# Three token tiles instead of two in the first rows of a feed-forward, and x of the third on another queue

## The chip, the cores and the metric

The kernel runs on one core of one Trainium2 chip. The metric is the device time of one execution in microseconds (us), the median over runs. A time shown with a profile is that of one profiled execution.

The engines are named as the profile names them: PE is TensorE's matmul stream and PEld its weight loads, DVE is VectorE, ACT is ScalarE, POOL is GpSimd, SP is SyncE, which here issues most DMAs. ACTq, POOLq and SPq are the queues on which those engines issue DMAs. Each engine runs its instructions in program order and waits at an instruction until its operands are ready, so what stands behind a waiting instruction waits too.

## The reference

Layer norm without weights over x (2048 tokens of 512 features), then the sum of three things: x, a diagonal complex state-space layer (S5) over the normalised tokens, and a SwiGLU feed-forward of them with 1376 hidden units. Inputs and output are bf16.

```python
x = A_x
xn = _layernorm(x, axis=-1)
return x + _A_ref(xn, ...) + _B_ref(xn, B_w_gate, B_w_up, B_w_down)

def _layernorm(x, axis=-1, eps=1e-5):
    m = jnp.mean(x, axis=axis, keepdims=True)
    v = jnp.var(x, axis=axis, keepdims=True)
    return (x - m) / jnp.sqrt(v + eps)

# _A_ref: Lam_bar = exp(dt * Lam);  B_bar = ((Lam_bar - 1) / Lam)[:, None] * Bmat
#         h_t = Lam_bar * h_(t-1) + B_bar @ xn_t
#         y_t = 2 Re(Cmat @ h_t) + xn_t * Dskip
# _B_ref: (silu(xn @ w_gate) * (xn @ w_up)) @ w_down
```

## The kernel before

**Tiles and chunks.** The 2048 tokens are 16 tiles of 128, four to a chunk, so four chunks of 512. Each chunk goes through the same stages on PE: `bproj` (L387, the projection of the normalised tokens by B, real and imaginary), the gate and up products of the feed-forward (L462 with hidden units on the partitions), `gateup_last` (L555, the 96 hidden units that don't fill a tile of 128), `out_ffn` (L630, the down product), `out_rest` (L620, its part for the last hidden units) and `out_ssm` (L643, the C product, added into the same PSUM bank). DVE does a rotation, a scan over time and a rotation back for each chunk (L397 to L411, L429), and the elementwise products of gate and up (L493, L541).

PE needs the tokens with features on the partitions. For chunks 1 to 3 they are normalised on DVE (chunk 1, L207) or ACT (chunks 2 and 3, L212) into `xn`, and one transposing DMA on SP (`xT_dma`, L262) turns all four tiles of a chunk into `xnT`. `bproj` of the chunk is the first to need it.

**The head.** Chunk 0 can't wait for that. Its first tiles are put through gate and up before the mean and deviation are known, with tokens as the stationary operand (`sw_mm`, L506): PE transposes raw x against an identity matrix (L237), adds minus the mean to the same PSUM bank by a matmul of the tokens' sums (`cT_mean`, L245), and ACT and DVE copy the result to `xcT` in bf16 (L252). The deviation comes in later, as the scale of the copies out of PSUM. Tiles 0 and 1 do this together, row by row of the weights as their DMAs land: `row_mm(0, k)` are the four matmuls of up for the rows k of the weights, `row_mm(1, k)` the gate's. Each weight row is a DMA of 256 KB on SP. Tile 2 comes later: it is centred on DVE (L226) once its statistics are there, and transposed into a bank `t2`. Tile 3 waits for a transposing DMA of its normalised tokens. What is left of the gate and up products of tiles 0 to 3 (hidden groups 0, 1 and 2 of 512, 512 and 352 units) is done in a loop over (group, tile), near L815, with L805 for the last group, whose gate and up share a bank.

**The parameters.** Lambda and log_dt come in as rows and are transposed on PE in one matmul (`prm_transpose`, L278), copied by DVE (`prm_copy`, L282), and lead to the tables of the rotation.

**The order of the work.** The program's order is written out by hand. Matmuls and what empties their banks are emitted in place. Statistics, normalisations, rotations, scans and table work go into a list, the backlog, with a cost in us for each, and `pump(us)` emits from the front of it as much as the credit `owed` allows. It is called beside each group of matmuls with about the time that PE needs for them. `need(tag)` emits all up to the last entry of a tag. Products are not in the backlog: they are emitted by `multiply(keep)`, which lowers the credit by 0.65 each. So the credit decides how the backlog's work stands between the products on DVE, between the copies out of PSUM on ACT, and so when each normalisation is done.

```python
def pump(us):
    owed[0] += us
    while backlog and owed[0] >= backlog[0][0] * 0.5:
        step()
```

The same mechanism holds the skip path at the end: `skip_op` makes `xr` on ACT (L592) and multiplies it on DVE (L600), for tiles 0 to 11, ahead of the back rotation of chunk 3. `out_ssm` copies a tile of chunks 0 to 2 out of PSUM on ACT into `res` (L652), which a DMA adds to the output in DRAM; for chunk 3 DVE adds it to x and the skip path (L646) and it is stored.

Of the kernel before, what the change touches and what calls it, by code (L numbers as in the profile page):

```python
# [11 lines left out]
BF16 = mybir.dt.bfloat16  # L12
ALU = mybir.AluOpType
# [10 lines left out]
def kernel(  # L24
# [17 lines left out]
    nc = tc.nc  # L42
    _, L, D = A_x.shape
# [6 lines left out]
    NCH = L // CW  # L50
    TPC = CW // 128
    KD = D // 128
# [15 lines left out]
    const = ctx.enter_context(tc.tile_pool(name="const", bufs=1))  # L68
# [9 lines left out]
    def bank(shape=(128, CW), dtype=F32):  # L78
        return psum.tile(list(shape), dtype, name="ps")
# [4 lines left out]
    x_v = A_x[0].rearrange("(n p) d -> p n d", p=128)  # L84
# [5 lines left out]
    xall = const.tile([128, NT, D], BF16, name="xall")  # L90
    xnT = const.tile([128, NCH, KD, CW], BF16, name="xnT")
# [38 lines left out]
    nc.scalar.dma_start(out=xall[:, 1, :], in_=x_v[:, 1, :])  # L130
# [43 lines left out]
    mv = const.tile([128, NT, 2], F32, name="mv")  # L174
# [30 lines left out]
    def norm_dve(n):  # L205
        c, i = divmod(n, TPC)
        nc.vector.tensor_scalar(out=xn_tile(c)[:, :, i, :], in0=by_k(xall[:, n, :]), scalar1=mv[:, n, 0:1],  # L207
                                scalar2=rstd[:, n:n + 1], op0=ALU.subtract, op1=ALU.mult)
# [8 lines left out]
    xcT, xc = CF[:, 0], CF[:, 1]  # L217
# [5 lines left out]
    sums = const.tile([128, 2], BF16, name="sums")  # L223

    def center(i):
        nc.vector.tensor_scalar(out=xc[:, i, :], in0=xall[:, i, :], scalar1=mv[:, i, 0:1], scalar2=None, op0=ALU.subtract)  # L226
# [5 lines left out]
    pair = [[[bank() for _ in range(2)] for _ in range(2)] for _ in range(2)]  # L232
    warm = pair[0][0][1]
    raw = [pair[0][1] + pair[1][0], pair[1][1] * 2]

    def cT_mm(ps, src, k, first, stop):
        nc.tensor.matmul(ps[:, k * 128:(k + 1) * 128], lhsT=src[:, k * 128:(k + 1) * 128], rhs=ident[:], start=first,  # L237
                         stop=stop)
# [5 lines left out]
    def cT_mean(i, *ks):  # L244
        nc.tensor.matmul(by_k(raw[i][ks[0]][:])[:, ks[0]:ks[-1] + 1:HK], lhsT=sums[:, i:i + 1].to_broadcast([128, 128]),  # L245
                         rhs=minus_mean[:, None, :].to_broadcast([128, len(ks), 128]), start=False, stop=True)

    def raw_copy(i, k):
        cT_copy(V.tensor_copy if k % 2 else nc.scalar.copy, raw[i][k], i, k, k + 1)

    def cT_copy(copy, ps, i, k0=0, k1=KD):
        copy(out=xcT[:, k0:k1, i * 128:(i + 1) * 128], in_=by_k(ps[:, k0 * 128:k1 * 128]))  # L252

    def runs(ap):
        return ap.rearrange("p k (i t) -> p (k i) t", t=128)
# [18 lines left out]
    V = nc.vector  # L274

    def prm_transpose():
        pp = bank()[:, 0:128]
        nc.tensor.matmul(pp, lhsT=prm_rows[:], rhs=ident[:], start=True, stop=True)  # L278
        return pp

    def prm_copy(pp):
        V.tensor_copy(out=prm[:].rearrange("p t q -> p (t q)"), in_=pp[:, 0:3 * NQ])  # L282

    def exp_pool(out, in_):
        nc.gpsimd.tensor_tensor(out=out, in0=e_t[:], in1=in_, op=ALU.pow)

    def params_a():
        V.tensor_tensor(out=dre[:], in0=dt_t[:], in1=lre, op=ALU.mult)
        exp_pool(r_t[:], dre[:])
        V.scalar_tensor_tensor(out=ws2[:, 0, :], in0=dt_t[:], scalar=INV_2PI, in1=lim, op0=ALU.mult, op1=ALU.mult)  # L290
# [212 lines left out]
    def sw_mm(ps, groups, gi, i, k0=0, k1=KD):  # L503
        a, b = fgroups[gi]
        for k in range(k0, k1):
            nc.tensor.matmul(ps[:, 0:(b - a) * 128], lhsT=tokens(i, k), rhs=groups[gi][:, k, 0:(b - a) * 128],  # L506
                             start=(k == 0), stop=(k == KD - 1))
# [14 lines left out]
    def sw_up(gi, i, psu):  # L522
        key, h, w = u_home(gi, i)
        if key not in u_pair:
            u_pair[key] = up_p.tile([128, 2, CW], BF16, name="u2")
        nc.scalar.activation(out=u_pair[key][:, h, 0:w], in_=psu[:, 0:w], func=ACT.Copy, scale=sw_scale(i))

    def sw_out(gi, i, psg, psu):
        a, b = fgroups[gi]
        key, h, w = u_home(gi, i)  # L530
        sw_gate(gi, i, psg)
        if psu is not None:
            sw_up(gi, i, psu)
        if h == 1:
            if key[-3:] == "g01":
                g = g0[:, 0:b, i, :].rearrange("p (h f) d -> p h f d", h=2)
                u = u_pair[key][:].rearrange("p h (f d) -> p h f d", d=128)
            else:
                g = g0[:, a:b, i - 1:i + 1, :]
                u = u_pair[key][:, :, 0:w].rearrange("p i (f d) -> p f i d", d=128)  # L540
            products.append(lambda: V.tensor_tensor(out=g, in0=g, in1=u, op=ALU.mult))  # L541
# [185 lines left out]
    dummy(warm, 4, CW)  # L727
    dummy(warm, 5, 128)
    nc.vector.tensor_scalar(out=minus_mean[:], in0=ident[:], scalar1=-1.0 / D, scalar2=None, op0=ALU.mult)
    for i in range(2):  # L730
        sum_dve(i, sums[:, i:i + 1])
    raw_mm(0)
    for k in range(HK):
        cT_mean(0, k)
        raw_copy(0, k)
    raw_mm(1)
    for k in range(HK, KD):
        cT_mean(0, k)
    for k in range(HK):
        cT_mean(1, k, k + HK)  # L740
        raw_copy(1, k)
    for k in range(HK, KD):
        raw_copy(0, k)
    for k in range(HK, KD):
        raw_copy(1, k)

    def row_mm(which, k):
        for i in range(2):
            for gi in range(2):
                sw_mm(pair[which][i][gi], (U, G)[which], gi, i, k, k + 1)  # L750

    for k in range(KD):
        row_mm(0, k)
    for i in range(2):
        ln_stats(i)
        ln_rstd(i, i + 1)
    for gi in range(2):
        for i in range(2):
            sw_up(gi, i, pair[0][i][gi])
    for n in range(2):  # L760
        norm_dve(n)
    row_mm(1, 0)
    pp = prm_transpose()
    ln_stats(2)
    center(2)
    ln_rstd(2, 3)
    ln_stats(3)
    ln_rstd(3, 4)
    prm_copy(pp)
    exp_pool(dt_t[:], ldt)  # L770
    for k in range(1, SW):
        row_mm(1, k)
    t2 = bank()
    for k in range(KD):
        cT_mm(t2, xc[:, 2, :], k, k == 0, k == KD - 1)
    cT_copy(nc.scalar.copy, t2, 2)
    row_mm(1, SW)
    for i in range(2):
        sw_out(0, i, pair[1][i][0], None)
    norm_dve(SW)  # L780
    xT0_dma(SW, TPC)
    norm_dve(2)
# [6 lines left out]
    for i in range(2):  # L789
        sw_out(1, i, pair[1][i][1], None)  # L790
    tables = table_ops()
    stats1, norm1 = ln_rest(1, False)
    queue("tables", tables[:1])
# [151 lines left out]
```

## Time and profile before

| What | us |
|---|---|
| median of 3 runs (lowest, highest) | 177.92 (177.83, 178.49) |
| the profiled execution's own time | 178.12 |
| its span in the profile | 176.0 |
| PE busy | 171.0 |
| DVE busy | 157.4 |
| ACT busy | 102.3 |
| POOL busy | 27.1 |

The span is the time from the first to the last record of the profile; the execution's own time has the start and end around it. The page gives shares of the span per engine, the busy tenths in 40 slices of 4.4 us each, the chain that ended last, followed backwards, and the costliest groups of instructions by line. The timeline lists the instructions of a stretch, one line for several of a kind: start, time from the first start to the last end, engine, line of the kernel, operation, output from input, count, and in brackets how long the engine stood idle before and what released it. In the list of DMA issues the last number is the time from issue to landing.

### The profile page before, as it was taken

What the parts mean: (1) busy time and instruction counts of PE and PEld (TensorE: products, weight loads), DVE (VectorE), ACT (ScalarE), POOL (GpSimd) and SP (SyncE); (2) the same over time, 40 slices, a digit from 0 to 9 for tenths busy, and PEclk for the clock granted to TensorE, in tenths of its full rate; (3) what the DMA queues carried; (4) which work ended last, traced back from release to release, by engine and by line L of the source; (5) the groups of instructions that cost most, each with busy time, mean ns of one, the idle gap of its engine ahead of it and who ended that gap; (6) DMA issues with size and microseconds to landing.
All of it is one profiled execution on the core that took longest, in us unless ns stands there. A gap on an engine that the chain in (4) does not pass through costs nothing.

```text
span 176.0 us, 2435 instructions
## 1 busy us (share of the span) xinstructions
PE 171.0 (97%) x878; PEld 82.0 (47%) x894; DVE 157.4 (89%) x260; ACT 102.3 (58%) x188; POOL 27.1 (15%) x36
## 2 busy tenths in 40 slices
PE   8899999999999999999999999999999999999993
PEld 5444445564444464444444444446444444444542
DVE  3767999999999999999999999999999999589642
ACT  3179589794996689976044362014666652983100
POOL 5234110022000000000302500014100000530700
PEclk9999999999999999999999999999999999999999
DMA  5998969999999300220005830006310000597741
GB/s 152 370 342 80 194 110 181 303 202 293 169 207 274 115 4 0 50 61 0 2 4 111 94 34 0 0 4 68 53 22 0 0 4 0 70 164 124 93 89 60
DMA packets 34027, 18.05 MB, mean 103 GB/s; under 512 B 24512, under 2 KB 32832, under 8 KB 33888
## 3 DMA queue, kind: packets, MB, share of 16 engines
q1 hardware_dynamic: 30272, 14.39, 35.0%
q0 software_dynamic: 3456, 3.28, 14.6%
q10 hardware_dynamic: 288, 0.23, 0.4%
q8 instruction: 7, 0.11, 0.3%
q14 instruction: 4, 0.03, 0.1%
HBM read 8.33 MB, written 5.24 MB: 77 GB/s over the span
## 4 chain that ended last, share of the span: by engine, by line
PE 94%; DMA 3%; issue 1%; SPq 0%; ACT 0%; DVE 0%; ACTq 0%
PE ps L462 29%; PE ps L630 20%; PE ps L643 16%; PE ps L387 16%; PE ps L506 7%; PE ps L555 3%; DMA wu<-in_B_w_up_dram 3%; PE ps L805 2%; PE ps L620 2%; ACT u L489 0%; SPq L122 0%; SPq L128 0%; DVE xall L646 0%; PE ps L237 0%; PE ps L278 0%
## 5 line engine op out<-in xcount | busy, mean ns | idle before, releaser
L429 DVE TENSOR_TENSOR_SCAN g<-r_t,car,u 128x512 bf16<-128x512 f32 x24 | 28.8, 1263 | 0.0
L643 PE MATMUL ps<-CF,wt 128*128 128x512 bf16 (+2 forms) x133 | 28.2, 366 | 0.2
L387 PE MATMUL ps<-xnT,BT 128*128 128x512 bf16 x125 | 28.1, 379 | 0.2
L630 PE MATMUL ps<-wd_sb,guT 128*128 128x512 bf16 (+2 forms) x129 | 26.5, 362 | 0.1
L462 PE MATMUL ps<-xnT,wu 128*128 128x512 bf16 x94 | 24.5, 379 | 0.2
L462 PE MATMUL ps<-xnT,wg 128*128 128x512 bf16 x93 | 24.3, 379 | 0.1
L389 ACT CAST u<-ps 128x512 bf16<-128x512 f32 x32 | 17.8, 591 | 5.0 <-PE ps L387 4.1
L489 ACT CAST u<-ps 128x512 bf16<-128x512 f32 x30 | 17.8, 592 | 4.8 <-PE ps L462 4.8
L643 PEld LDWEIGHTS <-wt 128*128 128x128 bf16 x136 | 12.9, 98 | 15.0 <-DVE xall L600 0.4
L387 PEld LDWEIGHTS <-BT 128*128 128x128 bf16 x128 | 12.5, 98 | 14.9 <-DMA BT<-in_A_B_re_dram 0.3
L630 PEld LDWEIGHTS <-guT 128*128 128x128 bf16 x130 | 12.4, 98 | 13.8
L199 POOL TENSOR_TENSOR rstd<-ve,neg_half 128x1 f32<-128x1 f32 (+1 forms) x7 | 7.0, 1001 | 73.0 <-DVE ve L198 72.6
L652 ACT CAST res<-ps 128x512 bf16<-128x512 f32 x12 | 6.9, 582 | 18.5 <-PE ps L643 18.5
L592 ACT ACTIVATE xr<-xall,nb,rstd 128x512 bf16<-128x512 bf16 x16 | 11.8, 804 | 8.7 <-DVE xall L600 5.0
L653 POOL DMA_DIRECT2D out_dram<-res x12 | 10.5, 1043 | 35.6 <-ACT res L652 30.0
L462 PEld LDWEIGHTS <-wu 128*128 128x128 bf16 x96 | 9.4, 98 | 11.3
L488 ACT ACTIVATE guT<-ps 128x512 bf16<-128x512 f32 x20 | 12.1, 604 | 4.0 <-PE ps L462 3.6
L462 PEld LDWEIGHTS <-wg 128*128 128x128 bf16 x96 | 9.3, 98 | 10.6
L212 ACT ACTIVATE xn<-xall,nb,rstd 128x512 bf16<-128x512 bf16 x8 | 6.3, 816 | 8.8 <-DVE nb L202 8.8
L189 DVE BATCH_NORM_STATS2 stats<-xall 128x6 f32<-128x512 bf16 x16 | 10.8, 675 | 0.6 <-DMA xall<-in_A_x_dram 0.6
L462 PE MATMUL ps<-xnT,w_end 128*128 128x512 bf16 x47 | 10.8, 379 | 0.1
L397 DVE TENSOR_TENSOR pm<-g,c 128x2048 bf16<-128x2048 bf16 x8 | 9.8, 1222 | 0.1
(132 smaller groups left out, 235.3 us busy)
## 6 DMA issues: line engine op xcount, KB each, us to landing
out_dram<-in_A_x_dram SPq DMA_DIRECT2D x8, 192.0 KB, 3.2
out_dram<-res POOLq DMA_DIRECT2D x12, 128.0 KB, 3.1
out_dram<-xall POOLq DMA_DIRECT2D x3, 512.0 KB, 6.4
wd_sb<-in_B_w_down_dram SPq DMA_DIRECT2D x1, 1280.0 KB, 7.8
wu<-in_B_w_up_dram SPq DMA_DIRECT2D x4, 256.0 KB, 4.9
wg<-in_B_w_gate_dram SPq DMA_DIRECT2D x4, 256.0 KB, 5.5
xall<-in_A_x_dram SPq DMA_DIRECT2D x1, 1024.0 KB, 7.0
xall<-in_A_x_dram SPq DMA_DIRECT2D x1, 512.0 KB, 6.1
```

What stands on the lines that cost most here:

```text
L189: nc.vector.bn_stats(out=stats[:, n, 0, :], in_=xall[:, n, :])
L387: nc.tensor.matmul(ps[:] if c else by_k(ps[:]), lhsT=BT[:, part, k, q * 128:(q + 1) * 128], rhs=xnT[:, c, k, :] if c else xnT0[:, k], star ...
L389: nc.scalar.copy(out=u_tiles[c][:, part, q, :], in_=ps[:])
L429: V.tensor_tensor_scan(out=g()[:, part, q, :], data0=r_t[:, q:q + 1].to_broadcast([128, CW]), data1=u_tiles[c][:, part, q, :], initial=ini ...
L462: nc.tensor.matmul(ps[:fs, lo:hi], lhsT=wslice(groups, fi, k), rhs=xnT[:, c, k, lo:hi], start=(k == 0), stop=(k == KD - 1))
L488: nc.scalar.activation(out=gu(c, fi, fi + 1)[:fs, 0, :], in_=psg[:fs], func=ACT.Silu)
L489: nc.scalar.copy(out=u_pair[c][:fs, fi % 2, :], in_=psu[:fs])
L506: nc.tensor.matmul(ps[:, 0:(b - a) * 128], lhsT=tokens(i, k), rhs=groups[gi][:, k, 0:(b - a) * 128], start=(k == 0), stop=(k == KD - 1))
L592: nc.scalar.activation(out=box["xr"][:], in_=xall[:, n, :], func=ACT.Identity, scale=rstd[:, n:n + 1], bias=nb[:, n:n + 1])
L630: nc.tensor.matmul(o_tiles[n, b][:, 0:hi - lo], lhsT=gu(c, fi, fi + 1)[:, 0, i * 128:(i + 1) * 128], rhs=wd_sb[:, fi, lo:hi], start=(fi == ...
L643: nc.tensor.matmul(o[:, 0:hi - lo], lhsT=w_tiles[c][:, part, q, i * 128:(i + 1) * 128], rhs=CF[:, part, q, lo:hi], start=False, stop=(part ...
L653: nc.gpsimd.dma_start(out=out_v[:, n, lo:hi], in_=res[:, lo:hi], accum_op=ALU.add)
```

## The change

The first three tiles go through the first rows together, where before it was two.

- **x of tile 2** is issued second on ACT's queue, right after x of tile 1. Before, it was issued on SP between the second and third gate rows.
- **Raw transposes.** Tiles 0 to 2 are all transposed raw, four matmuls each into one bank, and ACT copies them to `xrT` in SBUF in halves (six copies). The sums' matmul is one per tile (`mean_mm`) and writes minus the mean to a bank of its own. DVE adds the two into `xcT` (`centered`, nine instructions), so the subtraction that stood in PSUM is now in SBUF. The centring of tile 2, its bank `t2` and its four transposes are gone.
- **Up rows.** Row 0 of up is emitted in pieces between the centred columns, rows 1 to 3 for three tiles each, six matmuls. The gates follow tile by tile, all rows of a tile together.
- **Parameters.** The transpose of the parameters stands behind row 2 of up (`k == HK`), and `prm_copy` between the statistics of tile 0 and those of tiles 1 to 3.
- **The loop** over (group, tile) loses (0, 2) and (1, 2), with the `pump` beside each.

```diff
@@
-    nc.scalar.dma_start(out=xall[:, 1, :], in_=x_v[:, 1, :])
+    for i in (1, 2):
+        nc.scalar.dma_start(out=xall[:, i, :], in_=x_v[:, i, :])
     nc.scalar.preload_act_table_set("silu_and_others")
...
     for k in range(HK):
         load_row(nc.sync, wg01, wg_v, k)
-    nc.sync.dma_start(out=xall[:, 2, :], in_=x_v[:, 2, :])
     load_row(nc.sync, wg01, wg_v, HK)
@@
+    upb0 = [bank() for _ in range(2)]
+    raw = [bank() for _ in range(SW)]
+    low01, low2 = bank(), bank()
+    upb = [upb0, raw[0:2], [raw[2], bank()]]
+    gateb = [[low01, low2], upb[0], upb[1]]
+    warm = upb0[0]
+    xrT = xnT[:, NCH - 2]
...
     def raw_mm(i):
         for k in range(KD):
-            cT_mm(raw[i][k], xall[:, i, :], k, all(p is not raw[i][k] for p in raw[i][:k]), False)
+            cT_mm(raw[i], xall[:, i, :], k, k == 0, k == KD - 1)
...
+    def raw_copy(i, h):
+        k0, k1 = h * HK, (h + 1) * HK
+        nc.scalar.copy(out=xrT[:, k0:k1, i * 128:(i + 1) * 128], in_=by_k(raw[i][:, k0 * 128:k1 * 128]))
+
+    def mean_of(i):
+        return low2[:, 0:128] if i == SW - 1 else low01[:, i * 128:(i + 1) * 128]
+
+    def mean_mm(i):
+        nc.tensor.matmul(mean_of(i), lhsT=sums[:, i:i + 1].to_broadcast([128, 128]), rhs=minus_mean[:], start=i != 1,
+                         stop=i != 0)
+
+    def centered(i, k0, k1):
+        at = slice(i * 128, (i + 1) * 128)
+        V.tensor_tensor(out=xcT[:, k0:k1, at], in0=xrT[:, k0:k1, at],
+                        in1=mean_of(i)[:, None, :].to_broadcast([128, k1 - k0, 128]), op=ALU.add)
@@
     for i in range(2):
         sum_dve(i, sums[:, i:i + 1])
...
+    for i in range(2):
+        raw_mm(i)
+        mean_mm(i)
+        for h in range(2):
+            raw_copy(i, h)
+    raw_mm(2)
+    for h in range(2):
+        raw_copy(2, h)
+    for i in range(2):
+        centered(i, 0, 1)
+    sum_dve(2, sums[:, 2:3])
+    for gi in range(2):
+        up_mm(0, gi, 0)
+    up_mm(1, 0, 0)
+    mean_mm(2)
+    up_mm(1, 1, 0)
+    for i in (0, 2, 1):
+        for k in range(0 if i == 2 else 1, HK):
+            centered(i, k, k + 1)
+    for gi in range(2):
+        up_mm(2, gi, 0)
+    for i in range(SW):
+        centered(i, HK, KD)
+    for k in range(1, KD):
+        for i in range(SW):
             for gi in range(2):
-                sw_mm(pair[which][i][gi], (U, G)[which], gi, i, k, k + 1)
+                up_mm(i, gi, k)
+        if k == HK:
+            pp = prm_transpose()
+    for i in range(SW):
         ln_stats(i)
         ln_rstd(i, i + 1)
+        if i == 0:
+            prm_copy(pp)
+            exp_pool(dt_t[:], ldt)
+    for i in range(SW):
+        for k in range(KD):
+            for gi in range(2):
+                sw_mm(gateb[i][gi], G, gi, i, k, k + 1)
+        if i < 2:
+            for gi in range(2):
+                sw_up(gi, i, upb[i][gi])
     ln_stats(3)
     ln_rstd(3, 4)
+    for n in (0, 1, SW, 2):
+        norm_dve(n)
+        if n == SW:
+            xT0_dma(SW, TPC)
     xT0_dma(0, SW)
+    for gi in range(2):
+        sw_out(gi, 0, gateb[0][gi], None)
+    for gi in range(2):
+        sw_up(gi, SW - 1, upb[SW - 1][gi])
+    for gi in range(2):
+        sw_out(gi, 1, gateb[1][gi], None)
...
+    for gi in range(2):
+        sw_out(gi, SW - 1, gateb[SW - 1][gi], None)
@@
-    for gi, i in [(0, 2), (1, 2), (2, 0), (2, 1), (2, 2), (0, 3), (1, 3), (2, 3)]:
+    for gi, i in [(2, 0), (2, 1), (2, 2), (0, 3), (1, 3), (2, 3)]:
         sw_out(gi, i, *sw_both(gi, i))
         if (gi, i) == (2, 0):
             params_sin()
         pump(2 * KD * (fgroups[gi][1] - fgroups[gi][0]) * 128 / CW * 0.2163)
```

More of the change, by code (lines that the diff above doesn't have):

```diff
@@ L222 @@
     xn_c[0], xnT0 = rows_first(xc), rows_first(xnT[:, 0])
-    sums = const.tile([128, 2], BF16, name="sums")
-    def center(i):
-        nc.vector.tensor_scalar(out=xc[:, i, :], in0=xall[:, i, :], scalar1=mv[:, i, 0:1], scalar2=None, op0=ALU.subtract)
+    sums = const.tile([128, SW], BF16, name="sums")
     def sum_dve(i, dst):
@@ L230, in sum_dve @@
                                        in1=xall[:, i, HW:D], op0=ALU.mult, op1=ALU.add, accum_out=dst)
-    pair = [[[bank() for _ in range(2)] for _ in range(2)] for _ in range(2)]
-    warm = pair[0][0][1]
-    raw = [pair[0][1] + pair[1][0], pair[1][1] * 2]
+    upb0 = [bank() for _ in range(2)]
[5 more added lines that the diff above has]
+    xrT = xnT[:, NCH - 2]
     def cT_mm(ps, src, k, first, stop):
@@ L241, in raw_mm @@
         for k in range(KD):
-            cT_mm(raw[i][k], xall[:, i, :], k, all(p is not raw[i][k] for p in raw[i][:k]), False)
[L244 to L252, printed above, removed]
+            cT_mm(raw[i], xall[:, i, :], k, k == 0, k == KD - 1)
[11 more added lines that the diff above has]
+                        in1=mean_of(i)[:, None, :].to_broadcast([128, k1 - k0, 128]), op=ALU.add)
     def runs(ap):
@@ L729, with up_mm @@
     nc.vector.tensor_scalar(out=minus_mean[:], in0=ident[:], scalar1=-1.0 / D, scalar2=None, op0=ALU.mult)
+    def up_mm(i, gi, k):
+        sw_mm(upb[i][gi], U, gi, i, k, k + 1)
     for i in range(2):
         sum_dve(i, sums[:, i:i + 1])
[L732 to L748, printed above, removed]
+    for i in range(2):
[17 more added lines that the diff above has]
+            centered(i, k, k + 1)
@@ L749, in row_mm @@
+    for gi in range(2):
[4 more added lines that the diff above has]
+        for i in range(SW):
             for gi in range(2):
-                sw_mm(pair[which][i][gi], (U, G)[which], gi, i, k, k + 1)
-    for k in range(KD):
-        row_mm(0, k)
-    for i in range(2):
+                up_mm(i, gi, k)
+        if k == HK:
+            pp = prm_transpose()
+    for i in range(SW):
         ln_stats(i)
         ln_rstd(i, i + 1)
-    for gi in range(2):
-        for i in range(2):
-            sw_up(gi, i, pair[0][i][gi])
@@ L760 @@
[L760 to L766, printed above, removed]
+        if i == 0:
[8 more added lines that the diff above has]
+                sw_up(gi, i, upb[i][gi])
     ln_stats(3)
     ln_rstd(3, 4)
-    prm_copy(pp)
@@ L770 @@
[L770 to L782, printed above, removed]
-    xT0_dma(0, SW)
+    for n in (0, 1, SW, 2):
+        norm_dve(n)
+        if n == SW:
+            xT0_dma(SW, TPC)
+    xT0_dma(0, SW)
+    for gi in range(2):
+        sw_out(gi, 0, gateb[0][gi], None)
@@ L788 @@
                    allow_small_or_imprecise_dtypes=True)
-    for i in range(2):
-        sw_out(1, i, pair[1][i][1], None)
+    for gi in range(2):
+        sw_out(gi, SW - 1, gateb[SW - 1][gi], None)
     tables = table_ops()
```

2 lines of the change are left out of this document (1 added, 1 removed).

## The prediction

> **What bounds the kernel now.** I read the page first, for busy shares and the chain of waits, then the timeline around each place where the order of work changes.
>
> ```profile
> span 176.0 us, 2435 instructions
> PE 171.0 (97%) x878; PEld 82.0 (47%) x894; DVE 157.4 (89%) x260; ACT 102.3 (58%) x188; POOL 27.1 (15%) x36
> DVE  3767999999999999999999999999999999589642
> PE 94%; DMA 3%; issue 1%; SPq 0%; ACT 0%; DVE 0%; ACTq 0%
> ```
>
> TensorE works 171.0 of 176.0 us and holds 94% of the chain; no other engine has more than a few. So a change pays only by giving TensorE less to do or by an earlier start, and it costs whatever it makes TensorE wait for. DVE is full from the fifth slice to the 35th, so its order decides when things become ready.
>
> ```profile
> 3.09 0.61 PE L237 MATMUL ps<-ident,xall 128*128 128x128 bf16 x4
> 3.56 0.39 PE L245 MATMUL ps<-minus_mean,sums 128*128 128x128 bf16 x2
> 4.82 1.07 PE L506 MATMUL ps<-wu,CF 128*128 128x512 bf16 x4
> 6.49 2.75 PE L506 MATMUL ps<-wu,CF 128*128 128x512 bf16 x12 [0.60 <-DMA wu<-in_B_w_up_dram]
> 13.68 1.03 PE L506 MATMUL ps<-wu,CF 128*128 128x512 bf16 x4
> 14.54 1.03 PE L506 MATMUL ps<-wg,CF 128*128 128x512 bf16 x4
> PE ps L703 <- PEq L929: 0.8, 1, 0.8
> ...
> 0.90 0.37 ACTq L130 DMA_DIRECT2D xall<-in_A_x_dram  x1
> 1.20 1.83 SPq L122 DMA_DIRECT2D wu<-in_B_w_up_dram  x4
> ...
> wu<-in_B_w_up_dram SPq DMA_DIRECT2D x1, 256.0 KB, 4.8
> wu<-in_B_w_up_dram SPq DMA_DIRECT2D x1, 256.0 KB, 5.2
> ```
>
> In the timeline (start, length, engine, line) row 0 of the up weights is done at 5.9, and TensorE stands until 6.49 for row 1, whose load, the second of the four issued from 1.20 on, some 0.46 apart, took the 4.8 us of the DMA row: 1.65 + 4.8 = 6.45. Below it stands the fourth, 2.6 + 5.2 = 7.8. That 0.60 is all there is to win by waiting less at the head. One 128x512 matmul costs (14.54 - 13.68) / 4 = 0.215 us.
>
> **The change, part by part.**
>
> *Head.* Two matmuls of tile 2 join row 0 and are done before the stop: 2 x 0.215 = 0.43 us leave the work behind it. The four transposes of the centred tile 2 go too:
>
> ```profile
> L237 PE MATMUL ps<-ident,CF x4: 219/219/219, 11.7 to 11.9; 128*128 128x128 bf16 x4
> L252 DVE CAST CF<-ps x4: 280/286/291, 4.0 to 5.5; 128x128 bf16<-128x128 f32 x4
> 23.17 7.07 PE L387 MATMUL ps<-xnT,BT 128*128 128x512 bf16 x32
> L387 PEld LDWEIGHTS <-BT 128*128 128x128 bf16 x128 | 12.5, 98 | 14.9 <-DMA BT<-in_A_B_re_dram 0.3
> 31.40 1.89 PE L387 MATMUL ps<-xnT,BT 128*128 128x512 bf16 x7
> ```
>
> Four in about 0.22 us (an issue every 0.055). Against that, x of tile 2 (128 KB) now goes out on the Activation queue about 0.4 us after x of tile 1, ahead of rows 1 to 3 on the same engines. Rows 1 to 3 land (7.8 - 6.45) / 2 = 0.67 us apart at 256 KB each, so 128 KB cost some 0.34 and row 1 lands near 6.8. The other condition is DVE: nine additions from PSUM replace four casts; their price isn't in the trace. Bounds: the cast's issue interval of 0.2 us below, its 0.29 us of length above for a 128x128, twice that for the wide ones. I take the middle, 0.25, as the extra operand comes from SBUF. Before, the last of the four casts ended at 5.5 + 0.29 = 5.8; three columns more make 6.6 for the last that row 1 needs first. So row 1 starts at 6.85 (6.6 to 7.4) instead of 6.49. From there to the B projection TensorE needs 23.17 - 6.49 - 0.43 - 0.22 = 16.03 us: it arrives at 22.9, 0.3 us earlier (0.5 at best, 0.25 later at worst).
>
> *The parameter transpose* moves behind row 2 of the up weights, two rows of six matmuls after 6.85, so at 9.45; the DVE copy of it stands ahead of the statistics of tiles 1 to 3, which used to run before it. So the first transposing DMA can go out later, with BT behind it on SP: by 0 if DVE has time in hand there, by 1.3 (six matmuls) at most. BT was just in time before (weights of the B projection waited 0.3 us for it in the page's group), so that projection begins between 22.9 and 23.17 + 1.3 = 24.5; three statistics stay behind the copy, and I take 23.7. This gives up the head's gain and 0.5 more. Removing x of tile 2 from SP saves an issue of 0.4 us there, early, where SP has time.
>
> *Two credits are lost.* Elementwise work waits in a list from which `pump(us)` takes as much as TensorE time has been emitted. The loop over (group, tile) no longer holds (0, 2) and (1, 2); each carried 8 x 0.2163 = 1.73 us. Those matmuls still run, earlier, and nothing pumps for them. From there on the list runs 3.46 us behind TensorE, to its end. Products aren't in the list, so they now stand ahead of what they stood behind. It costs nothing where a result has that much slack. The three normalisations that feed `xT` and the end of the kernel are where it may not.
>
> Chunk 1, normalised on DVE:
>
> ```profile
> 21.15 0.68 DVE L541 TENSOR_TENSOR guT<-guT,u 128x1024 bf16<-128x1024 bf16 x1
> 21.75 0.69 DVE L309 TENSOR_SCALAR pm<-pm 128x1024 f32<-128x1024 f32 x1
> 23.69 1.38 DVE L207 TENSOR_SCALAR xn<-xall,mv,rstd 128x512 bf16<-128x512 bf16 x4
> 24.98 0.42 DVE L541 TENSOR_TENSOR guT<-guT,u 128x512 bf16<-128x512 bf16 x1
> 25.31 0.69 DVE L307 TENSOR_SCALAR pm<-pm 128x1024 f32<-128x1024 f32 x1
> xnT<-xn SPq DMA_TRANSPOSE x1, 4.3
> ```
>
> Ahead of the four normalisations there now stand a product of 1024 columns (0.60 to the next start, 21.15 to 21.75) and two of 512 (0.33 each, 24.98 to 25.31): 1.26 us. DVE is late already from the parameter copy (0 to 1.3) and the additions; I take 1.1. The last normalisation ends at 25.07 + 2.4 = 27.5, the DMA takes 4.3, so xT(1) lands at 31.85. TensorE was there at 31.5 before (the group begins 31.40; its first matmul's record is missing) and would be at 31.3: 0.35 us later than before. BT's lateness alone gives 0.5 for the same group, as the B projection and the last gate and up columns between them are solid. The later counts: 0.5, with 0 to 1.3 as bounds.
>
> Chunk 2, normalised on ACT between the gate and up pairs:
>
> ```profile
> 48.76 0.85 ACT L212 ACTIVATE xn<-xall,nb,rstd 128x512 bf16<-128x512 bf16 x1
> 49.48 0.62 ACT L488 ACTIVATE guT<-ps 128x512 bf16<-128x512 f32 x1
> 52.77 0.60 ACT L488 ACTIVATE guT<-ps 128x512 bf16<-128x512 f32 x1 [0.22 <-PE ps L462]
> 56.89 7.07 PE L387 MATMUL ps<-xnT,BT 128*128 128x512 bf16 x31
> ```
>
> Before, the fourth stood between pairs 4 and 5; now it stands behind pair 6. Pair 8's gate was ready at 52.7, pairs come 1.73 apart, so pair 6's up copy ends near 50.8, the fourth normalisation near 51.6 to 52.5, and xT(2) lands at 55.9 to 56.8 plus the 0.5 above. TensorE wants it at 56.9 plus the same: nothing lost, 0.5 at most.
>
> Chunk 3, normalised on ACT. This is the part that decides:
>
> ```profile
> 90.28 2.93 ACT L212 ACTIVATE xn<-xall,nb,rstd 128x512 bf16<-128x512 bf16 x4 [7.12 <-DVE nb L202]
> 96.18 0.58 ACT L652 CAST res<-ps 128x512 bf16<-128x512 f32 x1 [1.14 <-PE ps L643]
> 93.24 1.97 SPq L262 DMA_TRANSPOSE xnT<-xn  x1
> 92.52 7.08 PE L643 MATMUL ps<-CF,wt 128*128 128x512 bf16 x31
> 99.44 1.89 PE L387 MATMUL ps<-xnT,BT 128*128 128x512 bf16 x8
> ```
>
> Before, four normalisations stood together, ahead of the four copies of the output tiles (res) of chunk 0, and xT(3) went out at 93.24. In the changed order ACT has norm, res, norm, res, norm, norm, res, res. Each res waits for its tile's last matmul. So the third normalisation is queued behind the second res, which can't start before 96.18 however early the normalisations could have run. From there: res to 96.76, two normalisations at 2.93 / 4 = 0.73, the last with its tail 0.8, so the DMA goes out at 98.3 and lands 4.3 later, at 102.6. TensorE finishes the last tile of out_ssm at 99.44 and next needs xT(3). It waits 3.2 us. All these times shift together with anything lost before, so this term adds to it. Between the ends: if the two normalisations were free, it would wait 96.76 + 4.3 - 99.44 = 1.6; if the DMA also took the out-tile stores' traffic badly, 4.
>
> *The end.* The copies `xr` of the skip path now alternate with the res copies of chunk 2:
>
> ```profile
> 148.40 6.45 ACT L592 ACTIVATE xr<-xall,nb,rstd 128x512 bf16<-128x512 bf16 x9 [5.02 <-DVE xall L600]
> 155.23 2.35 DVE L397 TENSOR_TENSOR pm<-g,s 128x2048 bf16<-128x2048 bf16 x2
> 161.34 1.23 DVE L411 TENSOR_TENSOR wt<-pm 128x2048 bf16<-128x2048 bf16 x1
> 150.60 7.08 PE L643 MATMUL ps<-CF,wt 128*128 128x512 bf16 x31
> 165.62 6.64 PE L643 MATMUL ps<-CF,wt 128*128 128x512 bf16 x32
> ```
>
> Six xr, a res, five xr, a res, one xr: the second res waits for 150.60 + 2 x 1.73 = 154.06 (a tile of out_ssm is (99.44 - 92.52) / 4 = 1.73), the five xr behind the first res (152.3) end near 156.5, the twelfth xr near 157.7 and its product at 158.2, where DVE's back rotation of chunk 3 begins instead of 155.23. It takes 162.57 - 155.23 = 7.34 and ends at 165.5, as out_ssm(3) at 165.62 begins to need it. The cover of 3 us is used up; I take nothing, with 1.0 as the upper bound.
>
> Sum on the profiled execution's 178.12: 0.5 at xT(1), 0 at xT(2), 3.2 at xT(3), 0 at the end: 181.8. The runs' median is 0.2 below that execution, so 181.6.
>
> **A rule beside it.** The clock ran full after the head in every row above (128x512 at 0.215). At the head it was slow: four 128x128 in 0.47 us (3.09 to 3.56) against 0.22 later. The Trainium skill ("TensorE: Matmul & The Clock Gate", Part 1: The HAM clock gate) says that a TensorE idle for a whole free-running window of about 3.4 us falls back to half rate, and no wait of this trace after the head is long enough to test it. By that rule the stall forecast here, slightly shorter, would keep the clock; slightly longer, it might lose it.
>
> **The rivals.**
> 1. *The clock falls in the stall.* For: 3.2 us would be by far the longest idle time behind the head. At the head TensorE ran slow from the first dummy matmul (L703, at 0.8) to no later than 4.82, where four 128x512 take 1.07: 4 us at half rate, a loss of 2. Time: 183.6. Against: it would have to trip on this length. Chance 0.13.
> 2. *xT(3) costs half.* If the ACT work shrinks or the transfer, without BT or loads beside it, is faster, 1.6 us less: 180. Against: all three transposes of this form took 4.3. Chance 0.12.
> 3. *Not slower: the wait at xT(3) is hidden.* It decides at 99.44: if TensorE came to the end of out_ssm(0) later than to the second res by 3 us more than shown (held there by wt of chunk 0 or a slow store), the DMA would land in that time, and the head's gain would be all that's left. For: head 0.3, at best 0.65 if row 1 isn't delayed (0.43 + 0.22). Time 177.3 to 178.3. Against: four out_ssm tiles are back to back at 1.73 each, and each is only matmuls. Chance 0.15, a fifth of it faster.
>
> **How the numbers follow.** The forecast has 0.60: 180.8 to 182.8 (0 to 1.0 at xT(1), -0.5 to 0.3 at xT(3), 0 to 0.5 at xT(2)). Rivals 1 to 3 have the rest. The range 179.0 to 183.8 leaves out rival 3 and the upper edge of rival 1, some 0.2. A measurement of this kernel tells about 0.5% (0.9 us) from no change: faster 0.03, same 0.12, slower 0.85.
>
> **What would show it.** Row 1 starting at 6.6 to 7.4 with less than 0.6 idle; xT(1) issued near 27.5; on ACT the order norm, res, norm, res, norm, norm around 91 to 98, xT(3) issued near 98.7, and one PE idle time of about 3 us ahead of L387, put down to the DMA xnT. The forecast is wrong if that idle time is under 1 us, if the first matmuls after it run at half rate, or if DVE's back rotation of chunk 3 ends more than 1 us after out_ssm(3) could begin.

## The result, and the profile after

| What | before | after |
|---|---|---|
| median of 6 runs (lowest, highest), us | 177.88 (177.66, 178.49) | 186.83 (185.62, 188.19) |
| the profiled execution's own time | 178.12 | 186.06 |
| its span | 176.0 | 184.0 |
| PE busy | 171.0 | 174.4 |

The ratio is 1.0499, with a 95% interval of 1.044 to 1.0557: the kernel became 5% slower. The direction was forecast, the size (3.7 us) was less than half of what came, and the time lies outside the range of 179.0 to 183.8. Ratios, here and below, are of means and leave out executions more than 1.5% above the fastest of their kernel, which the medians and ranges keep.

From the page of the changed kernel: span, PE's busy time, the clock that was granted in each of 40 slices (in tenths), the chain that ended last, and the group of the B projection.

```profile
span 184.0 us, 2454 instructions
PE 174.4 (95%) x891; PEld 81.9 (44%) x891; DVE 159.0 (86%) x266; ACT 103.0 (56%) x189; POOL 27.4 (15%) x36
PEclk9999999999999999999999969999999999999999
PE 87%; DMA 8%; DVE 2%; ACT 0%; issue 0%; ACTq 0%; DVEq 0%
L394 PE MATMUL ps<-xnT,BT 128*128 128x512 bf16 x128 | 29.8, 394 | 5.3 <-DMA xnT<-xn 5.2
```

DMA took 8% of the chain, PE lost 7 points. One slice has its clock at 6 tenths: the 24th, from 105.8 to 110.4 us. And the B projection (now L394) has 5.3 us of idle time ahead of it, 5.2 of it ended by a transposing DMA. Its mean matmul grew from 379 to 394 ns. This execution has a mean granted clock of 0.991. The five others have 0.981 or 0.982, so their clock was low for about twice as long; none of them was profiled, but e5 below shows such an execution.

PE's timeline of the changed kernel (start, length, engine and line) at the places that the prediction went through:

```profile
5.05 0.61 PE L238 MATMUL ps<-ident,xall 128*128 128x128 bf16 x4 [0.53 <-DMA xall<-in_A_x_dram]
5.45 1.40 PE L513 MATMUL ps<-wu,CF 128*128 128x512 bf16 x3
6.69 0.22 PE L253 MATMUL ps<-minus_mean,sums 128*128 128x128 bf16 x1
...
7.36 3.19 PE L513 MATMUL ps<-wu,CF 128*128 128x512 bf16 x14 [0.23 <-DVE CF L258]
...
22.96 1.03 PE L818 MATMUL ps<-w_end,xnT 128*128 128x512 bf16 x4
24.15 7.08 PE L394 MATMUL ps<-xnT,BT 128*128 128x512 bf16 x32 [0.16 <-DMA BT<-in_A_B_re_dram]
...
32.85 7.08 PE L394 MATMUL ps<-xnT,BT 128*128 128x512 bf16 x32 [0.30 <-DMA xnT<-xn]
...
58.35 7.07 PE L394 MATMUL ps<-xnT,BT 128*128 128x512 bf16 x32
...
93.98 7.08 PE L650 MATMUL ps<-CF,wt 128*128 128x512 bf16 x32
105.93 8.60 PE L394 MATMUL ps<-xnT,BT 128*128 128x512 bf16 x32 [4.87 <-DMA xnT<-xn]
114.36 8.80 PE L637 MATMUL ps<-wd_sb,guT 128*128 128x512 bf16 x40
...
158.62 7.08 PE L650 MATMUL ps<-CF,wt 128*128 128x512 bf16 x32
...
173.64 6.64 PE L650 MATMUL ps<-CF,wt 128*128 128x512 bf16 x32
```

Against the starts of before, the lateness builds up ahead of the B projection of chunk 1 and around that of chunk 3, and nowhere else:

| stage begins | before | after | late by | new here |
|---|---|---|---|---|
| B projection of chunk 0 | 23.17 | 24.15 | 0.98 | 0.98 |
| B projection of chunk 1 | 31.40 | 32.85 | 1.45 | 0.47 |
| B projection of chunk 2 | 56.89 | 58.35 | 1.46 | 0 |
| out_ssm of chunk 0 | 92.52 | 93.98 | 1.46 | 0 |
| B projection of chunk 3 | 99.44 | 105.93 | 6.49 | 5.03 |
| down product of chunk 1, behind it | 106.34 | 114.36 | 8.02 | 1.53 |
| out_ssm of chunk 2 | 150.60 | 158.62 | 8.02 | 0 |
| out_ssm of chunk 3 | 165.62 | 173.64 | 8.02 | 0 |

So 1.5 us went at the head and up to chunk 1, 5.0 into one wait (4.87 of it shown as idle), 1.5 into slow matmuls behind that wait. The 32 matmuls that took 6.90 us before took 8.43.

ACT, SP, POOL and DVE of the changed kernel around the wait, each from its own timeline:

```profile
95.30 0.81 ACT L212 ACTIVATE xn<-xall,nb,rstd 128x512 bf16<-128x512 bf16 x1 [10.67 <-DVE nb L202]
96.02 0.56 ACT L659 CAST res<-ps 128x512 bf16<-128x512 f32 x1
96.48 0.81 ACT L212 ACTIVATE xn<-xall,nb,rstd 128x512 bf16<-128x512 bf16 x1
97.65 0.58 ACT L659 CAST res<-ps 128x512 bf16<-128x512 f32 x1 [0.35 <-PE ps L650]
98.13 1.52 ACT L212 ACTIVATE xn<-xall,nb,rstd 128x512 bf16<-128x512 bf16 x2
```

```profile
99.67 2.79 SPq L269 DMA_TRANSPOSE xnT<-xn  x1
```

```profile
96.89 0.95 POOL L660 DMA_DIRECT2D out_dram<-res  x1 [3.21 <-ACT res L659]
98.54 0.87 POOL L660 DMA_DIRECT2D out_dram<-res  x1 [0.70 <-ACT res L659]
100.41 0.86 POOL L660 DMA_DIRECT2D out_dram<-res  x1 [1.00 <-ACT res L659]
101.98 0.86 POOL L660 DMA_DIRECT2D out_dram<-res  x1 [0.71 <-ACT res L659]
```

```profile
95.13 0.14 DVE L202 SCALAR_TENSOR_TENSOR nb<-mv,rstd 128x4 f32<-128x4 f32 x1
```

The order on ACT is as forecast: norm, res, norm, res, norm, norm. The second res waits for PE (0.35), the last two normalisations follow it, and xT(3) goes out at 99.67. But the list of DMA issues in that stretch gives it 6.2 us to landing, not 4.3:

```profile
xnT<-xn SPq DMA_TRANSPOSE x1, 6.2
```

It now runs beside the stores of the res tiles, which POOL issues at 98.54, 100.41 and 101.98: while it is under way they move 0.39 MB. Before, it was issued at 93.24 and had landed by 97.54, when the stores had moved 0.03 MB. And nb, from which the normalisations start, came at 95.13 instead of 90.11, 3.6 us more than PE was late there (1.46).

### The profile page after: what moved, and what is told of

Read it like the earlier page. It is cut to its first block, busy times and chain, and to the rows that moved or that the text cites. A ratio compares the mean times of both kernels' runs of the same rounds, so it can differ in the third digit from the quotient of the medians.

```text
span 184.0 us, 2454 instructions
## 1 busy us (share of the span) xinstructions
PE 174.4 (95%) x891; PEld 81.9 (44%) x891; DVE 159.0 (86%) x266; ACT 103.0 (56%) x189; POOL 27.4 (15%) x36
## 4 chain that ended last, share of the span: by engine, by line
PE 87%; DMA 8%; DVE 2%; ACT 0%; issue 0%; ACTq 0%; DVEq 0%
PE ps L469 28%; PE ps L637 19%; PE ps L650 14%; PE ps L394 12%; PE ps L513 8%; DMA xnT<-xn 6%; PE ps L562 2%; DMA xall<-in_A_x_dram 2%; PE ps L818 2%; PE ps L627 2%; DVE xn L207 1%; DVE pm L317 1%; DVE pm L316 0%; PE ps L238 0%; DVE guT L548 0%
## 5 line engine op out<-in xcount | busy, mean ns | idle before, releaser
L394 PE MATMUL ps<-xnT,BT 128*128 128x512 bf16 x128 | 29.8, 394 | 5.3 <-DMA xnT<-xn 5.2
L394 PEld LDWEIGHTS <-BT 128*128 128x128 bf16 x128 | 12.6, 101 | 22.1 <-DMA xnT<-xn 5.9
L404 DVE TENSOR_TENSOR pm<-u,c 128x2048 bf16<-128x2048 bf16 x8 | 9.8, 1222 | 0.1
```

What stands on the lines that cost most here:

```text
L394: nc.tensor.matmul(ps[:] if c else by_k(ps[:]), lhsT=BT[:, part, k, q * 128:(q + 1) * 128], rhs=xnT[:, c, k, :] if c else xnT0[:, k], star ...
```

## The experiments

Twelve kernels were run. Times are medians. The kernel before was run beside each four of them (e1 to e4, e5 to e8, e9 to e12) on the same chip, at 177.7 to 177.8; across these groups the ratios are what can be compared.

| kernel | us (lowest to highest) | ratio to before, interval |
|---|---|---|
| the change | 186.83 (185.62, 188.19) | 1.0499 [1.044, 1.0557] |
| e1: credits back | 179.48 (178.72, 181.12) | 1.0124 [1.0059, 1.019] |
| e2: norms of chunk 3 first | 184.56 (182.54, 185.98) | 1.0341 [1.0273, 1.0409] |
| e3: dummies in the wait | 185.16 (183.95, 186.29) | 1.0412 [1.0343, 1.048] |
| e4: before, credits taken | 186.27 (185.91, 186.70) | 1.0476 [1.0445, 1.0508] |
| e5: stores emitted later | 186.81 (186.45, 187.47) | 1.0514 [1.0486, 1.0543] |
| e6: credits, dummies at the head | 178.66 (177.98, 179.51) | 1.0056 [1.0031, 1.008] |
| e7: credits, early parameters | 178.16 (177.44, 181.51) | 1.0028 [0.9999, 1.0057] |
| e8: before, x of tile 2 on ACT's queue | 177.63 (177.23, 178.30) | 0.9996 [0.9981, 1.0011] |
| e9: credits, tiles 0 and 1 first | 178.16 (177.41, 178.54) | 1.0025 [1.0011, 1.0039] |
| e10: stores held | 184.19 (182.28, 186.31) | 1.0328 [1.0284, 1.0373] |
| e11: credits, dummies, early parameters | 178.44 (177.85, 178.93) | 1.0041 [1.0021, 1.006] |
| e12: credits back late | 179.13 (178.27, 181.01) | 1.0071 [1.0046, 1.0097] |

### Is it the credits or the head? (e1, e4)

Two kernels from both sides: the change with the credits given back, and the kernel before with nothing but the credits taken away.

```diff
# e1, in the change
     multiply(1)
...
+    for _ in range(2):
+        pump(2 * KD * 0.2163)
+        multiply(1)
     for gi, i in [(2, 0), (2, 1), (2, 2), (0, 3), (1, 3), (2, 3)]:
# e4, in the kernel before
-        pump(2 * KD * (fgroups[gi][1] - fgroups[gi][0]) * 128 / CW * 0.2163)
+        if gi == 2 or i != 2:
+            pump(2 * KD * (fgroups[gi][1] - fgroups[gi][0]) * 128 / CW * 0.2163)
```

> The change, with the two lost credits given back: two calls of pump(1.73) ahead of the loop. Theory (the lost credits set the order on ACT, and that order makes the transposing DMA of chunk 3 late): the four normalisations of chunk 3 stand together again ahead of the res copies, xT(3) goes out before 97, PE has no idle time over 0.5 us ahead of the B projection of chunk 3, and its first matmuls run at 0.215 us. What stays is the head: 177.9 + 1.3 = 179.2 us, 178.7 to 180. Rival (the late start of DVE at the head alone makes everything late, the order doesn't matter): the wait stays, 185 to 187.

> The kernel before, whose loop skips pump(1.73) for (0, 2) and (1, 2); nothing else. Theory of the credits: ACT has norm, res, norm, res, norm, norm; the third normalisation waits for the second res at 96.2, xT(3) goes out at 98.3 and lands 4.3 to 6.2 later, 102.6 to 104.5; PE waits 3.2 to 5 us; with the clock falling by 1.5 at the longer wait: 181 to 184.5. Rival (the head's lateness): 177.9, not to be told from the kernel before.

e1 took 7.4 us back. e4, which has the old head untouched, is slower than before by 8.6 us, almost the whole of what the change lost, and above the 181 to 184.5 that was expected of it. PE's timeline of e4:

```profile
23.27 7.07 PE L387 MATMUL ps<-xnT,BT 128*128 128x512 bf16 x32
32.58 7.08 PE L387 MATMUL ps<-xnT,BT 128*128 128x512 bf16 x31 [0.92 <-DMA xnT<-xn]
...
105.86 8.57 PE L387 MATMUL ps<-xnT,BT 128*128 128x512 bf16 x31 [5.06 <-DMA xnT<-xn]
```

The B projection of chunk 0 begins within 0.1 us of before, so nothing is late at the head; then xT(1) costs 0.92, which the expectation didn't have, and xT(3) 5.06 and the clock, both at the upper end of what it had. The lost credits alone, without the new head, make nearly the whole loss. In e1 the line that answers to the last one has no wait:

```profile
100.08 7.07 PE L394 MATMUL ps<-xnT,BT 128*128 128x512 bf16 x31
```

The two effects don't add: a late xT(1) hides what the head lost before it, because both end in the same wait. With the old head e4 begins the B projection of chunk 1 at 32.58, the change at 32.85.

### Does the credit stay lost? (e12)

```diff
     queue_ssm(2)
+    for _ in range(2):
+        pump(2 * KD * 0.2163)
+        multiply(1)
     gateup_chunk(2)
```

> The change, with the two credits given back only ahead of the gate and up products of chunk 2. Theory (the credit is lost to the end until it is given back, and DVE's nb of chunk 3 at 95 comes from the c-coefficient copies standing late on ACT): these copies stand earlier again, nb near 91 to 92.5, four normalisations together, xT(3) out near 95, no wait at the B projection of chunk 3; the head's 1.3 us stay: 179.5. Rival (DVE is late from the head on): nb at 94 or later, xT(3) waits 2 us or more, 182 or more.

Given back only ahead of chunk 2's gate and up, some 50 us later, the credits cure it as well: 179.13. On DVE, nb of chunk 3 came at 91.19 and on ACT the four stood together:

```profile
91.37 2.93 ACT L212 ACTIVATE xn<-xall,nb,rstd 128x512 bf16<-128x512 bf16 x4 [7.90 <-DVE nb L202]
```

So the late nb of the change, 95.13, isn't DVE's lateness from the head: e12 has the same head, 1.1 us earlier in its profiled execution, and e4, with the old head and the credits lost, has nb at 94.86. How the lost credits do it is read from the traces, no run tries it alone: the eight copies of C coefficients (`cm`) on ACT alternate with gate and up copies in the change, and among DVE's waits is this one (us, times, longest), 2.6 of the 3.6 us:

```profile
DVE CF L380 <- ACT cm L377: 2.6, 5, 0.8
```

Neither the kernel before nor e12 has it in its list.

### Is the order on ACT the whole cause? (e2)

```diff
+        if c == 0:
+            need("ln3")
         need(f"ssm{c}")
         for n in range(c * TPC, (c + 1) * TPC):
             out_ssm(n)
```

> The change, with the four normalisations of chunk 3 emitted ahead of out_ssm of chunk 0, so ahead of its res copies; the credits stay lost. If the order on ACT is the whole cause, the wait is gone: about 180. If DVE, which gave nb of chunk 3 at 95.1 instead of 90.1, is half of it: norms 95.3 to 98.2, xT(3) out at 98.3, landing 102.7 if it takes 4.3 beside the first store, so PE waits 1.7 us, the clock stays full, and the time is 186.8 - 3.2 - 1.5 = 182 us. If it's DVE alone: 186 to 187.

It isn't. The four stood ahead of the res copies, began at 95.03 because nb came then, and xT(3) went out at 97.99. PE still waited:

```profile
104.14 8.46 PE L394 MATMUL ps<-xnT,BT 128*128 128x512 bf16 x31 [3.35 <-DMA xnT<-xn]
```

So a late nb suffices to make PE wait. That the late order does too is read from the change's trace, where the last two normalisations wait for the second res, and that one for PE (0.35), not for nb. The expected 182 was 2.5 too low: the wait was 3.35, not 1.7, as the transfer ran beside the stores and took 6.1, and in the profiled execution the clock fell after that too (8.46 instead of 7.07).

### The clock (e3)

```diff
     out_chunk(0)
+    dummy(bank(), 18, CW)
     bproj_chunk(3)
```

> The change, with 18 dummy matmuls of 128x512 (3.9 us, into a bank of their own) between out_ssm of chunk 0 and the B projection of chunk 3. They add nothing to the wait of 4.9 us for xT(3), as they fit in it. Theory (the clock fell because PE was idle): the B projection runs at 0.215 us from its first matmul, time 186.8 - 1.5 = 185.3 or less, and runs lie closer together than the 185.6 to 188.2 of the change. Rival (the first matmuls are slow for another reason, such as the stores or the arriving data): they stay at 0.427 us and the time at 186.8.

```profile
100.03 4.10 PE L710 MATMUL ps<-const-bfloat16-1.0 128*128 128x512 bf16 x18
105.31 7.08 PE L394 MATMUL ps<-xnT,BT 128*128 128x512 bf16 x31 [1.18 <-DMA xnT<-xn]
```

With PE kept busy the same 32 matmuls take 7.08 instead of 8.60 and the profile shows no slice with a lower clock. The wait itself is not shortened: 105.31 less the 6.91 from out_ssm's start at 93.11 leaves 5.3 us. The slow matmuls are the idle time's doing, for 1.5 us in the profile. The median is 1.7 lower, as expected, though the intervals of the two ratios overlap. The second half of the expectation failed: the runs still lie 2.3 us apart, so that spread isn't made here.

### The stores (e5, e10)

```diff
# e5: out_ssm keeps chunk 0's stores, and
     out_chunk(0)
     bproj_chunk(3)
+    for store in later:
+        store()
# e10: ahead of them, also
+    nc.gpsimd.tensor_tensor(out=hold[:], in0=xnT[:, 3, 0, 0:4], in1=xnT[:, 3, 0, 0:4], op=ALU.mult)
```

> The change, with the four accumulating stores of chunk 0's res tiles issued behind the B projection of chunk 3; the order on ACT and the lost credits stay. Theory (the transposing DMA took 6.2 us instead of 4.3 because the stores run beside it): xT(3) out near 99.7, 4.3 to landing, PE waits 3.1 us instead of 4.9: 185 us if the clock falls as it did after 3.35 us, 183.6 if it doesn't. Rival (the transfer is slow for another reason): 6.2 us and 186.8.

> The change, with POOL held by a small operation on the landed xT(3), so that the four stores of chunk 0's res tiles go out only after it. Theory (the transfer of xT(3) takes 6 to 7 us because these stores run beside it): 4.3 us from issue to landing, PE waits 3.1 instead of 4.9 to 5.7 us; 185 us if the clock still falls after 3.1 us, 183.6 if not. Rival (it is slow for another reason): 6 us or more, 186.8.

e5 tested nothing: POOL has no other work there, so stores emitted later in the program still go out as soon as their res tile is there (95.97, 97.62, 99.49, 101.05), and the transfer took 7.0 us. Its profile shows something else: after a wait of 5.69 us the B projection took 9.65, with the clock low for 6.8 us, where the change's profile has 8.60 and 3.4:

```profile
105.83 9.65 PE L394 MATMUL ps<-xnT,BT 128*128 128x512 bf16 x32 [5.69 <-DMA xnT<-xn]
```

In e10 POOL's small operation waits for xT(3), the stores follow at 104.90, and the list of DMA issues gives

```profile
xnT<-xn SPq DMA_TRANSPOSE x1, 4.3
```

PE's timeline of e10:

```profile
103.81 8.45 PE L394 MATMUL ps<-xnT,BT 128*128 128x512 bf16 x32 [2.95 <-DMA xnT<-xn]
```

The collision is shown: 1.9 us of the transfer, and 1.9 us of the wait. What is left, 2.95, is the order on ACT, within 0.3 of the predicted 3.2. And the clock fell again, though not in every execution: one of the four has a mean granted clock of 1.0, and 182.28 us, where the others have 0.990 or 0.991. In e2 it is the same, one of four, at 182.54.

### The head (e6, e7, e8, e9, e11)

All but e8 have the credits back, so that the head can be seen. e6 puts seven dummy matmuls ahead of tile 2's transposes, e7 moves the parameter transpose up by a row, e11 does both; e9 puts up row 0 of tiles 0 and 1 ahead of tile 2's transposes, and row 1 of both ahead of tile 2's own rows; e8 is the kernel before with x of tile 2 on ACT's queue.

```diff
# e6 and e11
+    dummy(upb[2][1], 7, 128)
     raw_mm(2)
# e7 and e11
-        if k == HK:
+        if k == 1:
             pp = prm_transpose()
# e8
-    nc.scalar.dma_start(out=xall[:, 1, :], in_=x_v[:, 1, :])
+    for i in (1, 2):
+        nc.scalar.dma_start(out=xall[:, i, :], in_=x_v[:, i, :])
...
-    nc.sync.dma_start(out=xall[:, 2, :], in_=x_v[:, 2, :])
# e9
+    dummy(upb[2][1], 5, 128)
...
+    for i in range(2):
+        for gi in range(2):
+            up_mm(i, gi, 0)
...
+    raw_mm(2)
+    mean_mm(2)
...
+    for i in range(2):
+        for gi in range(2):
+            up_mm(i, gi, 1)
...
+    for k in range(HK):
+        for gi in range(2):
+            up_mm(2, gi, k)
+    pp = prm_transpose()
```

> The kernel before, with only x of tile 2 moved to second place on ACT's queue. If its 128 KB push back row 1 of the up weights: PE's wait for row 1 grows from 0.60 to 0.95 us and the time to 178.2. If the rows don't mind: 177.8, wait 0.60.

e8 is the same as before, and its PE goes through rows 0 to 3 without the 0.60 for row 1:

```profile
4.92 3.62 PE L506 MATMUL ps<-wu,CF 128*128 128x512 bf16 x16
```

e4, where x of tile 2 is still on SP, hasn't that wait in its profile either, so the wait differs from one execution to the next, and a single profile can't price the move. The ratio can: its interval ends at 1.0011, 0.2 us, and the prediction took 0.34.

> The change with the two credits back, and seven dummy matmuls of 128x128 ahead of the raw transposes of tile 2, where PE stood 0.5 to 1.0 us waiting for x of tile 2. Theory (the change's runs differ by 2 us because that idle time lets the clock come up late in some of them): the runs lie within 0.6 us of each other, near the fast ones of 178.7; median 178.5 to 178.9. Rival (the spread is of the DMAs' arrival): median 179.5, runs still 178.7 to 181.

> The change with the two credits back, and the parameter transpose behind row 1 of up instead of row 2. Theory (DVE's late statistics come from its wait of 0.95 us for this transpose): DVE no longer waits there, the transposing DMA of tile 3 goes out 0.9 us earlier, PE doesn't wait for BT (0.2 us) nor for xT(1): 0.2 to 0.5 us under the kernel with the credits alone, so fast runs of 178.2 to 178.5. Rival (PE's own lateness at row 1 sets it): no difference.

> The change with the two credits back, seven dummies ahead of tile 2's raw transposes and the parameter transpose behind row 1, in the change's own order otherwise. If the two add up (the dummies took the spread of the runs, the parameters 0.3 us or more): median 178.0, spread 1 us. If the dummies don't hold the clock: median 178.2 and runs up to 180 or more, as with the parameters alone.

> The change with the two credits back, the parameter transpose behind row 1, and the head put in another order: up rows 0 and 1 of tiles 0 and 1 don't wait behind tile 2's raw transposes and sum, tile 2's rows 0 and 1 follow; five dummy matmuls of 128x128 ahead of row 0. Theory (what is left of the head's loss is PE's wait for x of tile 2 and for its column): no PE idle time over 0.3 us after 5 us, the B projection of chunk 0 begins near 22.6, the time is 177.2 to 177.7, not slower than the kernel before. Rival (BT's landing sets it whatever the head does): the B projection begins at 23.2, 178.0.

With the dummies (e6) the median is 178.66 against e1's 179.48, but the intervals of the ratios overlap; the eight runs lie 1.5 us apart, e1's four 2.4, and the 0.6 expected wasn't reached. The early parameter transpose (e7) gave 178.16, its fastest run 177.44, but with runs up to 181.51. Both together (e11) lie 1.1 us apart at 178.44, the narrowest of these, but the two don't add up in the median; the e6, e7 and e11 intervals overlap. e9's PE no longer waits for tile 2, yet its B projection of chunk 0 begins at 23.46, not near 22.6, and the time is above the 177.2 to 177.7 expected: in that execution row 0 of the weights was what it waited for.

```profile
5.51 1.02 PE L513 MATMUL ps<-wu,CF 128*128 128x512 bf16 x4 [1.08 <-DMA wu<-in_B_w_up_dram]
```

None of these beats the kernel before; e6, e9 and e11 stay 0.2 to 0.6% above it, with intervals clear of 1. The extra 0.65 us of matmuls that the three-tile head saves later are not to be seen in any of them.

## Why the prediction was right and wrong

**The lost credits and the order on ACT: right.** The mechanism that was put down as deciding is the one that decides. e4 shows that it needs nothing else of the change, e1 and e12 that giving the credits back removes it, e10 that with the stores held the order leaves a wait of 2.95 us, where 3.2 was predicted. The issue of xT(3) was forecast to 0.1 us: 98.3, shifted by the 1.46 lost before, against 99.67.

**The term of xT(3) was mis-sized, 3.2 against 5.0.** The step that failed is "the DMA goes out at 98.3 and lands 4.3 later". 4.3 was read from transfers of before, and xT(3)'s there had 0.03 MB of the stores beside it. Moved behind two res copies, the transfer meets the stores of these copies, 0.39 MB, and takes 6.2. The prediction named that traffic, as an upper end of 4 us, and chose 3.2 with a margin of 0.3 upwards, though the same sentence that moves the DMA puts the stores beside it. Rival 2 bet on the other direction and has nothing for it.

**The clock was left out of the sum and given 0.13.** Rival 1 happened, with 1.5 us instead of 2 in the profiled execution, and with it the prediction's own sign of being wrong, first matmuls at half rate. The Trainium skill ("TensorE: Matmul & The Clock Gate", Part 1: The HAM clock gate) has an idle window of about 3.4 us, and the prediction leaned on its stall being shorter. In the change the wait was 4.87; but e10 shows the clock falling after a wait of 2.95 us in all, where the measurement and the rule part. The low stretch itself lasted 3.4 us in the change (105.6 to 109.0), e2, e4 and e10, and 6.8 in e5. By their mean clocks, five of the change's six executions are like e5, which lost 2.6 us to it, so in the median this term is likely nearer to 2.6 than to the profile's 1.5. With the wait at 3.2 as predicted, it should have been in the forecast: e10 is that case, it kept its clock in one execution of four, and it stands at 184.2, outside the range as well.

**The head and xT(1): predicted 0.5, measured 1.45.** Row 1 was to begin at 6.85 and not after 7.4. The first 7.36 in the timeline is tile 2's part of row 0, two matmuls of 0.216, so row 1 began at 7.79. The price of DVE's additions was right (a single column takes 0.28 us, and one begins every 0.21 to 0.24). What was missed is PE's queue: tile 2's transposes stand ahead of up row 0, and x of tile 2 came 0.53 us later than PE; the sum of tile 2 stands behind three matmuls of row 0, and DVE waited for it until 7.01. These three ran at 0.427 (5.45 + 1.40), at half the clock until 6.6, where before it was full from 4.9. That last part is not the new head's doing: e4 has the old head and no such idle time, and its sixteen matmuls of up took 4.44 us from 4.90 on, where e8's took 3.62. It differs from one execution to the next: in the profiles with the change's head and the credits lost up to there, the B projection of chunk 0 begins between 23.02 (e12) and 24.15, against 23.17 before, so the 0.98 of this profile is the upper end. The parameter copy held DVE for 0.95 us until PE got to row 2, as was read; what that costs in time isn't settled, as e11 and e6, which differ in it alone, can't be told apart. The credits' part in the wait for xT(1) was too small: e4 waits 0.92 us where 0.35 was worked out, and with the old head begins the B projection of chunk 1 1.18 us late.

**DVE's nb at 90.1 plus a small lag: wrong, without effect here.** It came 5 us late, half of that beside the waits for `cm`. Since the second res bound ACT anyway, it changed nothing in this kernel; in e2, where the order was mended, it and the transfer beside the stores made 3.35 us.

**Chunk 2 and the end: right.** Nothing was lost at xT(2) (1.45 to 1.46), and out_ssm of chunk 3 is as late as chunk 2's, 8.02. DVE's back rotation of chunk 3, forecast from 158.2, began at 166.24, which is 158.2 and the 8.0 lost before. **Rival 3, not slower, had no part.**

**What stays open.** What sets the spread of the runs at the head: it is narrower in e6 and e11, but the time at which the clock comes up and the order in which x and the first rows land both vary between executions, and no run separates them. What decides whether the clock falls in a wait near 3 us, and for how long, is open too: it fell in three executions of four in e10 and in e2, and no kernel was tried with a wait between 1.2 and 2.95 us there.

## What to carry to other kernels

Where a hand-kept credit decides how elementwise work is laid between matmuls, moving matmuls without moving their credit shifts every later decision: look for the first consumer whose slack is smaller than the shift, here some 80 us further on. When a transfer is moved, price it at its new place, beside what is issued there, not at its old duration. And where PE waits for some 3 us, count the half-rate matmuls behind it as likely: here they came in three executions of four.

## What the runs showed of the hardware

- A transposing DMA of 16 blocks took 4.3 us with at most 0.04 MB of the accumulating stores' data moved beside it (before, e1, e10, e12), 6.1 with 0.27 MB (e2), and 6.2, 6.4 and 7.0 with 0.39 MB (the change, e4, e5).
- PE's clock fell after an idle time of 2.95 us (e10), 3.35 (e2), 4.87 (the change), 5.06 (e4) and 5.69 (e5). It stayed low for 3.4 us and cost 1.4 to 1.5, in e5 for 6.8 us and 2.6: seven 128x512 matmuls at 0.427 us in the change, then 0.216 again. Without the idle time (e3) it stayed. The page of the Trainium skill named above puts the idle window at about 3.4 us; two of these waits are shorter than that.
- x of one tile put on the ACT queue, ahead of 256 KB weight rows on SP's, cost no more than the 0.2 us to which the interval of e8 reaches.
- At the head the matmuls ran at the full rate from 4.9 us before the change and from 6.6 in it. In e12's profile the four transposes at 3.50 already took 0.39 us, at full rate, where the change's took 0.63, and in e4, with the old head, the full rate came at 6.5: the moment varies from one execution to the next.
